# Threshold attention and Fourier mixing on one core: transposing the next pair's q and k one step earlier in the first two batches, and scaling its q at a step's end in the second

## The chip, the cores and the metric

The kernel runs on one core of a Trainium2 chip. The metric is the device time of one execution in microseconds (us). Of the kernel before there are three timed executions: 1657.55, 1662.69 and 1664.34 us, with the median 1662.69. The execution in the profile took 1657.76 us by the clock of the run and 1655.7 us from its first to its last instruction; all times "at 185.94" below are microseconds from the start of that span. A core has four engines that compute, each with its own queue: TensorE (PE, matmuls and transpositions through matmuls), VectorE (DVE), ScalarE (ACT) and GpSimd (POOL). A fifth, SyncE (SP), issues nearly all the DMAs here.

## The reference

Eight batches of eight heads, 576 tokens, 64 values a head. Scores below the row's maximum less tau are dropped before the softmax. Its output is the input of a Fourier mixing (the real part of a two-dimensional transform over tokens and over the 512 values), a normalization and two matmuls with a relu between them.

```python
scores = scale * np.matmul(q, k.transpose(0, 1, 3, 2))
thresh = np.max(scores, axis=-1, keepdims=True) - tau
scores = np.where(scores >= thresh, scores, -1000000000.0)
attn = np.exp(scores - np.max(scores, axis=-1, keepdims=True))
attn = attn / (np.sum(attn, axis=-1, keepdims=True) + 1e-09)
x = np.matmul(attn, v)                     # then (B,H,S,D) -> (B,S,H*D)
u = x + np.real(np.fft.fft(np.fft.fft(x, axis=1), axis=2))
un = (u - mean(u)) / np.sqrt(var(u) + 1e-06)
out = u + np.maximum(un @ w_ch1, 0.0) @ w_ch2
```

All arithmetic is in 32-bit floating point. The two weight matrices arrive as 64-bit values and are converted on the chip.

## The kernel before

**Pairs and steps.** Heads are worked on two at a time: 4 pairs a batch, 32 in all, numbered n. A pair has NT = 5 steps t = 0 to 4. In the first four a step takes 128 queries of both heads; the fifth (t = 4) takes the last 64 queries of both heads at once, from a small tile `q_ends`. So a batch is 20 steps (`per_batch`), and step i is step t = i mod 5 of pair n = i div 5.

**One step.** `scores` (L420) multiplies q and k into one or two PSUM tiles `sc`, of which there are two in all; L430 is the matmul of the first four steps, with the column half c in the outer loop and the head j in the inner one, L436 that of the fifth. `softmax` (L442) then takes the negated row maximum `neg` (L453, DVE), the exponential `e` (L461, ACT), the threshold `thr` (L465, ACT), the masked exponential with its row sum (L469, DVE, the last reader of the `sc` tile), and the reciprocal of the sum (L481, DVE). In the first two batches the reciprocal is spread into `rec` on GpSimd (L493). `weights_in_parts` (L504) transposes `e` on TensorE (L533, L536, L552) and ScalarE copies the result out (L540, L544, L554, L556). `weighted_values` (L561) multiplies with v, in two parts a pair (L581; L589 scales the result).

**Preparing the next pair.** `load_pair` (L124) issues eight DMAs that bring q and k of a pair, in blocks, into the tiles `q_in` and `k_in`, of which there is one each. `scale_q` (L384; L390 on GpSimd) multiplies `q_in` by 1/8. `prep_pair` (L394) makes the layout that the score matmuls want by three block transpositions on VectorE: L401 and L402 write `kT` (two buffers), L404 writes `qT` (one buffer); then it calls `load_pair` for the pair after. `prep_ends` (L409; L413 on GpSimd) copies the last 64 queries from `qT` to `q_ends`.

**Who sets the order.** In the first two batches the order of every engine is that of the program text, as the manual schedule is open from L101 to L1385. The first batch runs `step` (L1177) for i = 0 to 19. There `prep_pair(n + 1)` stands in the fifth step, after that step's `softmax`. Each step also takes one chunk of the first weight matrix through its conversion (L297 and L300 on DVE, L305, L308, L311 on ACT, L313 on DVE, L318 and L319 on GpSimd), and `busy` (L105) puts in matmuls that nobody reads. The second batch runs `second_batch` (L1313) for i = 20 to 39. It converts the second weight matrix by a list of chunks (`PLAN`), calls the Fourier mixing of the first batch (`mixing`, L653) and feeds its rows to the two matmuls of the last part (`channels`, L823, with L814 and L840) in portions: `fill` (L1161) takes as many portions as a budget allows. In its steps from the fourth on a call of `fill` stands before `transposed_weights(i - 1)`, one after the chunk stages, and one after that `prep_pair`. From the third batch on (L1388) only TensorE follows the text; a scheduler orders the other engines. There `prep_pair` stands at t = 3 already, and that loop is not touched.

In the second batch's step 22 (t = 2 of pair 4) `mix` sends GpSimd the last six additions of the Fourier mixing (L723 and L727), whose results the first matmuls of the last part (L814) need.

Of the kernel before, what the change touches and what calls it, by code (L numbers as in the profile page):

```python
# [47 lines left out]
def kernel(  # L48
# [18 lines left out]
    NT = 5  # L67
# [37 lines left out]
    def busy(n):  # L105

        for _ in range(n):
            pd = ps.tile([128, 4, 128], FP32, tag="mm", bufs=4, name="pd")
            four = bass.AP(
                tensor=ones.tensor, offset=ones.offset, ap=[list(ones.ap[0]), [0, 4], [1, 128]]  # L110
            )
            nc.tensor.matmul(pd[:, :, :], ones[:, :], four, start=True, stop=True)
# [31 lines left out]
    def load_v(n):  # L144

        b, p = n // NPAIR, PAIRS[n % NPAIR]
        vt = v_in[n % 2]
        for j in range(2):
            h = 2 * p + (j + p) % 2
            nc.sync.dma_start(  # L150
                out=vt[:, j:8:2, :], in_=v[b, h, 0:512, :].rearrange("(t p) d -> p t d", p=128)
            )
            nc.sync.dma_start(out=vt[64 * j : 64 * j + 64, 8 + j, :], in_=v[b, h, 512:576, :])
# [230 lines left out]
    def scale_q(n):  # L384

        raw = loaded[n][0]
        if n == 0:
            nc.scalar.activation(out=raw[:, :], in_=raw[:, :], func=ACT.Copy, scale=q_scale[:, :])
        else:
            nc.gpsimd.tensor_scalar(  # L390
                out=raw[:, :], in0=raw[:, :], scalar1=q_scale[:, :], scalar2=None, op0=ALU.mult
            )
# [16 lines left out]
    def prep_ends(n):  # L409

        for j in range(2):
            hp = slice(64 * j, 64 * j + 64)
            nc.gpsimd.tensor_copy(q_ends[hp, hp], heads[n][0][hp, 512:S])  # L413
# [6 lines left out]
    def scores(i):  # L420
        n, t = divmod(i, NT)
        qT, kT = heads[n][0:2]

        nh = 2 if t < 4 else 1
        sc = [ps.tile([128, 2, 512], FP32, tag="sc", name=f"sc{j}") for j in range(nh)]
        if t < 4:
            for c in range(2):
                for j in range(2):
                    hp, k0 = slice(64 * j, 64 * j + 64), D * (1 - j)
                    nc.tensor.matmul(  # L430
                        sc[j][:, c, 0:HALF], qT[hp, 128 * t : 128 * t + 128],
                        kT[hp, k0 + HALF * c : k0 + HALF * (c + 1)], start=True, stop=True,
                    )
        else:
            for c in range(2):
                nc.tensor.matmul(  # L436
                    sc[0][:, c, 0:HALF], q_ends[:, :], kT[:, D + HALF * c : D + HALF * (c + 1)],
                    start=True, stop=True,
                )
        steps[i] = (sc, nh)  # L440
# [59 lines left out]
    def transposed_weights(i):  # L500
        for _ in weights_in_parts(i):
            pass
# [58 lines left out]
    def weighted_values(n, part):  # L561

        b, p = n // NPAIR, PAIRS[n % NPAIR]
        _, _, vt, e_t, ends, recs = heads[n]
        m = (256, S - 256)[part]
        if n % NPAIR == 0 and part == 0:

            xs[b] = [None] * NPAIR
            x = xs[b][p] = sb.tile([128, m], FP32, tag="half", bufs=1, name="x_first")
        else:  # L570
            x = xs[b][p]
            if x is None or n % NPAIR == 0:
                x = sb.tile([128, S], FP32, tag=f"x{p}", bufs=1, name=f"x{p}")
            if n % NPAIR == 0:
                nc.gpsimd.tensor_copy(x[:, 0:256], xs[b][p][:, :])
            xs[b][p] = x
        cols = slice(256 * part, 256 * part + m)
        pv = ps.tile([128, 512], FP32, tag="mm", bufs=4, name="pv")
        for c in range(5):
            for j in range(2):  # L580
                nc.tensor.matmul(  # L581
                    pv[64 * j : 64 * j + 64, 0:m], vt[:, 2 * c + j, :],
                    e_t[:, 4 * j + c, 0:m] if c < 4 else ends[:, 0:m],
                    start=(c == 0), stop=(c == 4), skip_group_check=True,
                )
        if normalized(n):
            nc.scalar.copy(x[:, cols], pv[:, 0:m])  # L587
        else:
            nc.vector.tensor_tensor(  # L589
                out=x[:, cols], in0=pv[:, 0:m], in1=recs[:, 0:m], op=ALU.mult  # L590
            )
        if part == 0:
            return
        heads.pop(n)
        if p % 2:

            swap = sb.tile([2, S], FP32, tag="half", bufs=1, name="swap")
            for j in range(2):
                nc.sync.dma_start(out=swap[j : j + 1, :], in_=x[64 * j : 64 * j + 1, :])
            for j in range(2):  # L600
                nc.sync.dma_start(out=x[64 * j : 64 * j + 1, :], in_=swap[1 - j : 2 - j, :])
# [575 lines left out]
    def step(i):  # L1177

        n, t = divmod(i, NT)
        scores(i)  # L1180

        def last_stages():
            run = chunks.pop(i - 1, None)
            for _ in range(2 if run else 0):
                next(run, None)

        if t == 1 and n > 0:
            softmax(i, lambda: weighted_values(n - 1, 1), last_stages)
            load_v(n + 1)
        elif t == 3:  # L1190
            softmax(i, lambda: weighted_values(n, 0), last_stages)
        else:
            softmax(i, None, last_stages)
        if t == 1 and n > 0:
            pass
        elif later and later[0][0] <= i:
            later.pop(0)[1](i)
        else:
            busy(2 if i < NCHUNK else 1)
        if t == 2:  # L1200
            scale_q(n + 1)
        if t == NT - 1:
            prep_pair(n + 1)
        if t == 1:
            prep_ends(n)
        if i in chunks:
            next(chunks[i])
        if i > 0:
            transposed_weights(i - 1)
        if i in chunks:  # L1210
            next(chunks[i])
        while after and after[0][0] <= i:
            after.pop(0)[1]()
        if i > 0 and i + 3 < NCHUNK:
            chunks[i + 3] = w1_chunk(i + 3)
        if t == 2 and n > 0:
            folds.append(fold_rows(n - 1))
        if folds and next(folds[0], True):
            folds.pop(0)
# [93 lines left out]
    def second_batch(i):  # L1313

        nonlocal budget
        n, t = divmod(i, NT)
        first = i - per_batch
        if first != 1:
            scores(i)
        if first == 0:  # L1320

            transposed_weights(i - 1)
        softmax(i, None, lambda: (advance(first - 1), advance(first - 1)))
        chunks.pop(first - 1, None)
        transfers(first)
        fold_more()
        if t == 1:
            prep_ends(n)
        if t == 2:
            scale_q(n + 1)  # L1330
        if first == 0:
            weighted_values(n - 1, 1)
            scores(i + 1)
            column_means(LAST)
            copy_mean(LAST)
            folds.append(fold_rows(n - 1))
            while folds:
                fold_more()
            load_v(n + 1)
            start_batch(0)  # L1340
            mix(3)
            mix(3)
        elif first == 1:
            mix(3)
            transposed_weights(i - 1)
            mix(2)
            mirrored(LAST)
            for c, eng in ((1, nc.vector), (3, nc.vector), (0, nc.gpsimd), (2, nc.gpsimd)):
                less_mean(eng, LAST, c)
            advance(first)  # L1350
            advance(first)
        elif first == 2:
            mix(2)
            transposed_weights(i - 1)
            mix(2)
            weighted_values(n, 0)
            advance(first)
            advance(first)
        else:
            fill()  # L1360
            transposed_weights(i - 1)
            advance(first)
            advance(first)
            fill()
            if t == 4:
                prep_pair(n + 1)
            fill()
            if t == 2:
                weighted_values(n, 0)
            if t == 0:  # L1370
                weighted_values(n - 1, 1)
                folds.append(fold_rows(n - 1))
                load_v(n + 1)
        if first == 16:
            fold_halves(1)
        if first < 3:
            budget += 3 * per_slot
# [10 lines left out]
    for i in range(2 * per_batch, total + 1):  # L1388
# [4 lines left out]
        n, t = divmod(i, NT)  # L1393
# [79 lines left out]
```

## Time and profile before

| | us | share of the span |
|---|---|---|
| span of the profiled execution | 1655.7 | |
| TensorE busy | 1584.1 | 96% |
| VectorE busy | 1170.7 | 71% |
| ScalarE busy | 820.9 | 50% |
| GpSimd busy | 660.1 | 40% |
| one transposition L401 or L404 (128x576), median | 0.769, 0.768 | |
| one L402 (64x64), at 229.57 | 0.24 | |
| one scaling L390 in the first two batches, median | 1.73 | |

The chain of work that ended last lies on TensorE for 77% of the span, on VectorE for 14%, on ScalarE for 5% and on GpSimd for 1%. The first two batches are its mixed part: the step t = 0 of pair 8, the first of the third batch, has its scores at 305.04.

A line of a timeline gives the start, the duration, the engine, the line of the program, the operation, the tile written and the tiles read, and in brackets how long the engine had been idle before it and what ended that idle time. Adjacent matmuls of one line are merged. A line of the window table gives, for one stretch of time, how long each engine was busy.

### The profile page before, as it was taken

To read this page: it belongs to the slowest core of one execution; us is meant where nothing else is said; L and a number is where in the kernel's file an instruction comes from. 1 tells how busy PE (TensorE), PEld (TensorE's weight loads), DVE (VectorE), ACT (ScalarE), POOL (GpSimd) and SP (SyncE) were. 2 spreads that over 40 slices of the span, in tenths; PEclk is the share of its full clock that TensorE was granted. 3 is DMA by queue.
4 is the path that set the end of the run, shared out by engine and by line. 5 is a ranking of instruction groups with operands and counts; after the bars stand their busy time and mean duration, and the time that the engine had idled before them with its cause. 6 is when DMAs were issued, how large, how long until landed. Compare 5 with 4: busy or idle time off the path is not lost.

```text
span 1655.7 us, 27993 instructions
## 1 busy us (share of the span) xinstructions
PE 1584.1 (96%) x10346; PEld 1248.7 (75%) x10346; DVE 1170.7 (71%) x2518; ACT 820.9 (50%) x1786; POOL 660.1 (40%) x875
## 2 busy tenths in 40 slices
PE   8888878999999999999999999999999999999998
PEld 4545445557888787878888778887888788889998
DVE  7986776667768678776676768787786868664444
ACT  5764566444535464645353556454646455532111
POOL 6773565141431525225333253424342244215232
PEclk9999989999999999999999999999999999999999
DMA  6423221211011111100101010111101110000000
GB/s 158 122 55 111 56 83 42 43 28 29 12 35 20 25 26 29 36 16 21 28 16 35 15 35 16 42 22 22 29 15 43 22 28 1 14 4 11 13 14 14
DMA packets 203086, 57.43 MB, mean 35 GB/s; under 512 B 193827, under 2 KB 193829, under 8 KB 202950
## 3 DMA queue, kind: packets, MB, share of 16 engines
q1 hardware_dynamic: 200438, 55.34, 14.2%
q8 instruction: 82, 1.34, 0.3%
q10 hardware_dynamic: 2512, 0.30, 0.1%
q14 instruction: 54, 0.44, 0.1%
HBM read 46.02 MB, written 9.44 MB: 33 GB/s over the span
## 4 chain that ended last, share of the span: by engine, by line
PE 77%; DVE 14%; ACT 5%; issue 2%; POOL 1%; DVEq 0%; ACTq 0%; POOLq 0%
PE ph L918 23%; PE po L1082 20%; PE pv L581 9%; PE sc L430 8%; PE pw L552 5%; PE po L840 3%; DVE e L469 3%; DVE neg L453 2%; PE ph L814 2%; ACT e L461 2%; PE sc L436 1%; PE py L684 1%; PE pn L774 1%; PE pa L701 1%; DVE hs L1043 1%
## 5 line engine op out<-in xcount | busy, mean ns | idle before, releaser
L453 DVE TENSOR_REDUCE neg<-sc 128x1 f32<-128x576 f32 x288 | 207.5, 749 | 174.2 <-PE sc L430 159.9
L461 ACT ACTIVATE e<-sc,neg 128x576 f32<-128x576 f32 x288 | 212.2, 737 | 229.1 <-DVE neg L453 228.7
L469 DVE SCALAR_TENSOR_TENSOR e<-sc,thr,e 128x576 f32<-128x576 f32 x288 | 229.5, 813 | 50.5 <-ACT thr L465 49.0
L1082 PE MATMUL po<-w,hs 128*128 128x256 f32 x1024 | 246.9, 384 | 0.0
L1082 PEld LDWEIGHTS po<-w,hs 128*128 128x128 f32 x1024 | 186.7, 191 | 33.9 <-issue 12.9
L430 PE MATMUL sc<-kT,qT 64*128 64x288 f32 x1024 | 169.3, 434 | 35.0 <-DVE qT L404 27.7
L918 PE MATMUL ph<-u_t,w 128*128 128x128 f32 x1536 | 187.0, 276 | 0.0
L918 PEld LDWEIGHTS ph<-u_t,w 128*128 128x128 f32 x1536 | 179.1, 192 | 5.0 <-issue 3.7
L552 PE MATMUL pw<-ident,e 128*128 128x128 f32 x1152 | 171.2, 276 | 8.0 <-ACT y_o L689 2.3
L554 ACT COPY e_t<-pw 128x512 f32<-128x512 f32 x256 | 148.7, 594 | 49.8 <-PE pw L552 49.5
L430 PEld LDWEIGHTS sc<-kT,qT 64*128 64x128 f32 x1024 | 93.8, 188 | 98.3 <-issue 35.2
L552 PEld LDWEIGHTS pw<-ident,e 128*128 128x128 f32 x1152 | 135.7, 142 | 27.3 <-issue 4.2
L927 DVE TENSOR_TENSOR hs<-ph,hs 128x512 f32<-128x512 f32 x160 | 106.9, 685 | 69.5 <-PE ph L918 53.8
L918 PE MATMUL ph<-t_u,s_w 128*128 128x128 f32 x1024 | 126.4, 277 | 2.2 <-POOL t_u L892 1.8
L918 PEld LDWEIGHTS ph<-t_u,s_w 128*128 128x128 f32 x1024 | 119.5, 192 | 7.7 <-issue 4.9
L1082 PE MATMUL po<-hs,s_tile 128*128 128x256 f32 x512 | 121.5, 381 | 0.0
L796 DVE SCALAR_TENSOR_TENSOR u<-po,rstd,u 128x256 f32<-128x256 f32 (+1 forms) x164 | 75.3, 483 | 63.9 <-PE po L1082 62.9
L488 ACT ACTIVATE e<-e,den 128x576 f32<-128x576 f32 x96 | 74.5, 776 | 75.7 <-DVE den L481 75.3
L1082 PEld LDWEIGHTS po<-hs,s_tile 128*128 128x128 f32 x512 | 94.1, 190 | 13.7 <-issue 2.5
L935 ACT ACTIVATE hs<-hs 128x512 f32<-128x512 f32 x112 | 69.2, 630 | 62.1 <-DVE hs L927 62.1
L614 POOL TENSOR_TENSOR half<-x 128x287 f32<-128x287 f32 x48 | 40.5, 865 | 115.6 <-ACT x L587 61.0
L1078 POOL TENSOR_TENSOR hs<-hs,s_tile 128x512 f32<-128x512 f32 x32 | 42.1, 1318 | 109.4 <-PE po L1082 86.5
(196 smaller groups left out, 2911.2 us busy)
## 6 DMA issues: line engine op xcount, KB each, us to landing
hs<-in_moe_w_ch_dram SPq DMA_DIRECT2D x23, 512.0 KB, 4.5
q_in<-in_q_dram SPq DMA_DIRECT2D x128, 72.0 KB, 2.4
out_dram<-u SPq DMA_DIRECT2D x36, 256.0 KB, 2.1
k_in<-in_k_dram SPq DMA_DIRECT2D x124, 72.0 KB, 2.3
v_in<-in_v_dram SPq DMA_DIRECT2D x64, 128.0 KB, 2.3
w<-in_moe_w_ch_dram SPq DMA_DIRECT2D x6, 512.0 KB, 3.7
stage<-in_moe_w_ch_dram SPq DMA_DIRECT2D x3, 512.0 KB, 3.5
v_in<-in_v_dram SPq DMA_DIRECT2D x64, 16.0 KB, 2.1
```

The source lines that it names most:

```text
L430: nc.tensor.matmul(sc[j][:, c, 0:HALF], qT[hp, 128 * t : 128 * t + 128], kT[hp, k0 + HALF * c : k0 + HALF * (c + 1)], start=True, stop=True,)
L453: nc.vector.tensor_reduce(out=neg[:, j : j + 1], in_=sc[j][:, :, 0:HALF], axis=AXIS_XY, op=ALU.max, negate=True,)
L461: nc.scalar.activation(out=ej, in_=sc[j][:, :, 0:HALF], func=ACT.Exp, bias=neg[:, j : j + 1], scale=1.0)
L469: nc.vector.scalar_tensor_tensor(out=ej, in0=sc[j][:, :, 0:HALF], scalar=thr[:, j : j + 1], in1=ej, op0=ALU.is_ge, op1=ALU.mult, accum_out ...
L488: nc.scalar.activation(out=e[:, S : 2 * S], in_=e[:, S : 2 * S], func=ACT.Copy, scale=den[:, 1:2])
L552: nc.tensor.transpose(pw[:, c, :], e[:, c0 : c0 + 128], ident[:, :])
L554: nc.scalar.copy(e_t[:, 4 * j : 4 * j + 4, qs], pw[:, :, :])
L581: nc.tensor.matmul(pv[64 * j : 64 * j + 64, 0:m], vt[:, 2 * c + j, :], e_t[:, 4 * j + c, 0:m] if c < 4 else ends[:, 0:m], start=(c == 0), ...
L796: nc.vector.scalar_tensor_tensor(out=u, in0=product, scalar=self.rstd[:, t : t + 1], in1=u, op0=ALU.mult, op1=ALU.add,)
L918: nc.tensor.matmul(banks[name][:, 128 * q : 128 * q + 128], left[c][:, 512 * part + 128 * q : 512 * part + 128 * q + 128], right[c], start ...
L927: nc.vector.tensor_tensor(out=to, in0=bank, in1=to if other is None else other, op=ALU.add)
L1082: nc.tensor.matmul(bank[:, 0 : DM // 2], left[p], right[p], start=start and p == 0, stop=p == NK - 1, skip_group_check=True,)
```

## The change

Three edits, no operation added or taken away. In the first batch `prep_pair(n + 1)` moves from the fifth step (t = 4) to the fourth (t = 3), so that on VectorE the three transpositions stand before the fifth step's softmax instead of after it. In the second batch the same is done: the call moves from t = 4 to t = 3 at the same place inside a step, after the chunk stages and before the last `fill`. And in the second batch `prep_ends` and `scale_q` move from just after the step's softmax to the end of the step, behind whatever else that step gives to GpSimd. The purpose is to have `qT` ready before the next pair's first scores are due, and to let GpSimd do what others wait for first.

```diff
@@ step: first batch
         if t == 2:
             scale_q(n + 1)
-        if t == NT - 1:
+        if t == 3:
             prep_pair(n + 1)
@@ second_batch
         fold_more()
-        if t == 1:
-            prep_ends(n)
-        if t == 2:
-            scale_q(n + 1)
         if first == 0:
...
             fill()
-            if t == 4:
+            if t == 3:
                 prep_pair(n + 1)
             fill()
...
                 load_v(n + 1)
+        if t == 1:
+            prep_ends(n)
+        if t == 2:
+            scale_q(n + 1)
         if first == 16:
```

As `prep_pair` also loads the pair after, its eight DMAs move up in SyncE's queue with it, past one load of a weight chunk where one stands there. TensorE's order is the same in both kernels. From the third batch on a few small instructions of VectorE and ScalarE near the batch's beginning change places, because the scheduler is given another situation.

## The prediction

> **What bounds the kernel now.** I read the page first, then who waits for L404, then the windows from one pair's first scores to the next pair's, then the timelines of three engines at those boundaries. From the page, part 5:
>
> ```profile
> L430 PE MATMUL sc<-kT,qT 64*128 64x288 f32 x1024 | 169.3, 434 | 35.0 <-DVE qT L404 27.7
> ```
>
> TensorE stands idle 27.7 us in the whole run because a score matmul waits for `qT`. The line of L404, asked from 0 to 420 us alone, says where:
>
> ```profile
>   PE sc L430: 27.7, 8
> ```
>
> All 27.7 us lie in the first two batches, eight times, once for each of the pairs 1 to 8. The windows (core, engine busy times with their counts, clock granted to TensorE, DMA share) tell what those stretches are bound by:
>
> ```profile
> 39.40:70.30 30.90, 26.91 (x142) 15.52 (x142) 27.70 (x64) 23.57 (x52) 23.71 (x30) 1.00 0.43 115
> 101.30:132.20 30.90, 24.33 (x132) 14.67 (x132) 25.33 (x55) 18.61 (x43) 20.90 (x27) 0.94 0.16 30
> 185.90:230.60 44.70, 32.60 (x170) 20.12 (x170) 37.60 (x76) 29.90 (x70) 28.86 (x33) 0.91 0.30 79
> 270.60:305.00 34.40, 31.91 (x158) 18.60 (x158) 19.40 (x48) 14.68 (x37) 13.37 (x22) 0.95 0.19 35
> 305.00:340.00 35.00, 34.36 (x169) 18.43 (x170) 22.50 (x58) 18.70 (x42) 2.19 (x3) 1.00 0.23 44
> ```
>
> In the first batch VectorE (27.70 of 30.90) is fuller than TensorE; in the second they alternate; from pair 7 on TensorE leads, and after 305 it is busy 34.36 of 35.00. So time gained before 305 reaches the end undiminished, but time that TensorE alone gains in the first batch need not. The waits of the second batch in TensorE's timeline:
>
> ```profile
> 171.61 2.93 PE L814 MATMUL ph<-u_t,w 128*128 128x384 f32 x4 [3.59 <-POOL u_t L727]
> ...
> 185.94 1.24 PE L430 MATMUL sc<-kT,qT 64*128 64x288 f32 x8 [2.88 <-DVE qT L404]
> ...
> 230.66 2.29 PE L430 MATMUL sc<-kT,qT 64*128 64x288 f32 x8 [8.47 <-DVE qT L404]
> 232.88 4.51 PE L814 MATMUL ph<-u_t,w 128*128 128x384 f32 x8
> ...
> 270.60 2.29 PE L430 MATMUL sc<-kT,qT 64*128 64x288 f32 x8 [3.35 <-DVE qT L404]
> ...
> 305.04 1.24 PE L430 MATMUL sc<-kT,qT 64*128 64x288 f32 x8 [2.52 <-DVE qT L404]
> ```
>
> After the idle times of 3.35 us and more the same eight score matmuls take 2.29 us instead of 1.24, and eight of L814 4.51 instead of 2.75 (at 237.88): an idle stretch is paid twice. GpSimd's timeline ahead of 171.61:
>
> ```profile
> 164.84 1.92 POOL L390 TENSOR_SCALAR q_in<-q_in,q_scale 128x576 f32<-128x576 f32 x1
> 166.73 0.85 POOL L723 TENSOR_TENSOR u_t<-x,tmp 128x289 f32<-128x289 f32 x1
> ...
> 170.87 0.69 POOL L727 TENSOR_TENSOR u_t<-x,tmp 1x287 f32<-1x287 f32 x1
> ```
>
> The scaling of q stands without a gap before the additions that TensorE waits for. And VectorE's before 230.66:
>
> ```profile
> 225.04 0.16 DVE L481 RECIPROCAL den<-den 128x1 f32<-128x1 f32 x1
> ...
> 229.82 0.78 DVE L404 STREAM_TRANSPOSE qT<-q_in 128x576 f32<-128x576 f32 x1
> ...
> 232.98 1.42 DVE L453 TENSOR_REDUCE neg<-sc 128x1 f32<-128x576 f32 x2 [2.38 <-PE sc L430]
> ```
>
> Between softmax and transpositions stand two chunks' conversions, so the scores come 5.8 us after their tile was free (224.81), and then VectorE waits for them too.
>
> **What the Trainium skill says.** "TensorE: Matmul & The Clock Gate", Part 1, says that the clock falls to half after an idle window of about 3.4 us, that the windows run freely, and that about 3.4 us of activity bring it back; its Part 4 says that transpositions on TensorE do not count as activity in the same way. The trace agrees roughly: 3.35, 3.59 and 8.47 us of idleness were followed by halved speed, 2.52, 2.88 and 2.96 were not; and at 198.39 L814 is slow (4.45) after 3.3 us in which only transpositions ran. Its section "Architectural detail" says that VectorE and ScalarE work strictly in order and that TensorE pulls only weight loads forward. The trace agrees: at 229.82 L404 sits behind conversions, though its inputs were there. So a moved instruction delays all behind it in its queue.
>
> **The change part by part.** No operation is added. The price of the moved group is 0.77 + 0.24 + 0.78 less overlaps, 1.85 us as at 229.82 (228.79 to 230.60); L401 and L404 took 0.756 to 0.779 in all 64 cases, whatever ran beside, so it is the same in the new place.
>
> Behind the transpositions on VectorE now come the fifth step's chunk stages, its `neg`, then e on ScalarE and L469. The next pair's second score matmul (c outer, j inner) needs the `sc` tile that the fifth step's L469 frees; so the wait for `qT` becomes a wait for that L469, 2.3 us earlier in the queue than the end of L404 (129.96 against 132.2 for pair 4), later by what the transpositions push it.
>
> *Pairs 1 to 3.* VectorE is continuous through the fourth and fifth steps, so L469 is pushed by the whole 1.85 us. Pair 2: `neg` of t = 0 was at 71.59, right behind L300; it stays there. Pair 3 likewise (102.86). Pair 1 had 0.68 us of waiting for the scores at 40.68, and I get 40.2. Together 0.5 us.
>
> *Pair 4.* No chunks; VectorE is idle 1.11 us before the fifth `neg` (127.32). Transpositions from 126.2 to 128.05 push it by 0.73; L469 ends at 130.7 instead of 129.96; scores then, instead of 132.27: 1.5 gained. The PV matmuls at 135.45 took 5.5 us instead of the usual 2.9 (idle since 129); if the clock stays up, 2.6 more.
>
> *Scaling last, step 22.* L390 (1.92) leaves the place before the additions, the copies of `q_ends` (0.52, from 152.74, where they cost nothing as GpSimd idles 1.40 before 155.57) go into that gapless row: 1.4 earlier, and 1.4 more if L814 at 171.61 (2.93 instead of 1.56 at 166.46) runs at speed. L390 then ends at about 172, before the transpositions of step 23 want it at 174. The same move later in the batch hides in GpSimd's gaps (6.3 and 5.1 us at 180.93 and 189.38).
>
> *Pair 5.* The transpositions fall into VectorE's idle 5.28 us before 178.53: free. TensorE could go at 183.07 instead of 185.94 (2.9), but ScalarE is busy with conversions to 185.8, where e could have its turn, against 188.01: 2.2 gained.
>
> *Pair 6.* The transpositions push the fifth `neg` by 1.85, but ScalarE was late for it (222.97 against 221.5), so L469 moves by only 0.5, to end at 225.3. Scores at 225.4; VectorE does its two chunks to 229.25 and reads them; ScalarE is free at 231.5 instead of starting at 233.77; its copies for the PV matmuls no longer wait 2.06 us for L814 and end at 235.2. PV at 235.2 instead of 240.56: 5.3, of which about 2.8 is the slow clock.
>
> *Pair 7.* The fifth `neg` at 265.7 instead of 263.77, e pushed by 1.3 (a table load held ScalarE until 265.34), scores at 268.5 instead of 270.60: 2.1, and 1.2 from the clock: 3.3.
>
> *Pair 8.* VectorE idles 1.67 us before 299.74: pushed by 0.2. TensorE is free at 302.5, scores at 302.95 instead of 305.04: 2.1.
>
> *DMAs.* Loads of q and k are issued a step earlier, one chunk load behind them about 5 us later (SyncE issues eight in 4.3 us, at 39.38). The chunk so delayed is wanted some 6 us or more after it lands (from 2.4 to 4.5 us a load on the page). Nothing.
>
> Sum: 0.5 + 4.1 + 2.8 + 2.2 + 5.3 + 3.3 + 2.1 = 20.3 us, of which 2.6 + 1.4 + 2.8 + 1.2 = 8.0 depends on the clock. As its windows run freely, a drop may come elsewhere; I take 60% of that: 12.3 + 4.8 = 17.1.
>
> **The rivals.** *VectorE is the bound.* Then TensorE's earlier scores only wait for `neg` and e, and of the gains only those of pairs 7 and 8 remain, where VectorE has 15 us to spare: 5.4 us less, 1657. For it: 37.60 of 44.70 us for pair 5. Against it: VectorE itself waited 1.33 to 2.38 us for these scores.
>
> *The wait moves and grows (slower).* If nothing comes back because t = 0 waits for the fifth step's L469, and each of eight fifth steps is pushed by 1.85: 14.8 us, 1677; with the pushes of pairs 1 to 3 and half the others, about 1673. Against it: L469's end is before L404's in all eight.
>
> *Everything falls.* The eight waits vanish wholly, with the clock and GpSimd's part: 27.7 + 8.0 + 1.4 = 37 us, 1626. Against it: the `sc` tile is not free sooner.
>
> **How the numbers follow.** My forecast 75 in 100, VectorE as the bound 12, slower 5, everything 8. The likeliest: 1662.7 - 17.1 = 1645.6, so 1646. Low 1636: the whole sum with the clock (1642.4) and something of the third rival, less the spread of the median. High 1656: the gain without the clock (1650) and half the way to the first rival. Faster by over 0.5% (below 1654.4) is nearly all of the forecast and the third rival, 0.82; no change 0.12; slower 0.06.
>
> **What would show it.** The wait on L404 should all but vanish for pairs 1 to 8, and one on L469 of about half its size take its place; the fifth `neg` of pairs 1 to 3 should come 1.8 us later. The wait for L727 should fall from 3.59 to about 2.2, the clock's eights in the page's slices become nines, pair 8's first scores come near 288, and the time from there to the end stay at 1350.7. It is wrong if the waits reappear at `neg` and `thr` with the boundaries unmoved, or if the third batch, scheduled anew, loses what was gained.

## The result, and the profile after

| | median, us | against the kernel before on the same chip | mean clock lost a run, us |
|---|---|---|---|
| kernel before, beside the first comparison | 1662.79 (1657.55 to 1664.34) | | 22.8 |
| the change | 1635.97 (1635.02 to 1638.93) | 0.9847 [0.9822, 0.9872] | 6.5 |
| the change, once more beside later experiments | 1638.08 (1635.44 to 1638.85) | 0.9860 [0.9845, 0.9874] | 8.6 |

The last column is used below: one minus the mean granted TensorE clock, times the span. For the kernel before it is the mean of the 63 executions that stood beside the experiments.

By medians the change makes the kernel 22.5 to 26.8 us faster. The forecast was 16.7 faster, to 1646, and 1636 was the lower end of its range: the direction is right, the size too small by about a third. The profiled execution spans 1633.3 us, 22.4 less than before; the profile of the kernel before is of one of its faster executions (1657.76).

From the page of the kernel after, parts 1, 2 and 5:

```profile
PE 1580.4 (97%) x10346; PEld 1247.5 (76%) x10346; DVE 1171.1 (72%) x2518; ACT 821.4 (50%) x1786; POOL 661.8 (41%) x875
...
PEclk9999999999999999999999999999999999999999
...
L430 PE MATMUL sc<-kT,qT 64*128 64x288 f32 x1024 | 173.3, 430 | 14.5 <-DVE e L469 13.7
```

The work is the same (VectorE 1171.1 us busy, 1170.7 before). TensorE's score matmuls stood idle 14.5 us instead of 35.0, and what ends most of that is no longer `qT` but the masked exponential L469. The clock row of the page before had a single eight, which is gone:

```profile
PEclk9999989999999999999999999999999999999999
```

TensorE's idle time fell from 71.6 to 52.9 us (span less busy), its busy time by 3.7: these two make the 22.4.

Who waited for L404 after, again from 0 to 420 us:

```profile
  PE sc L430: 0.7, 1
```

Of eight waits one is left. Waits on L469 in that stretch grew from 6.6 us (12 times) to 13.2 (21 times), so 20.4 us less in all. The windows from one pair's first scores to the next pair's, the same five as before:

```profile
38.90:69.40 30.50, 27.37 (x144) 15.72 (x144) 27.41 (x64) 23.54 (x53) 22.08 (x29) 1.00 0.46 120
100.60:128.60 28.00, 24.07 (x134) 14.25 (x134) 23.79 (x55) 18.41 (x44) 21.28 (x27) 1.00 0.13 25
174.00:213.70 39.70, 33.15 (x175) 20.65 (x174) 34.88 (x73) 28.65 (x68) 26.06 (x31) 1.00 0.34 87
250.40:283.00 32.60, 31.14 (x160) 17.99 (x159) 21.25 (x54) 16.20 (x41) 13.92 (x24) 1.00 0.22 41
283.00:318.00 35.00, 34.03 (x164) 17.94 (x164) 22.07 (x58) 19.55 (x45) 2.02 (x2) 1.00 0.18 37
```

The first stretch is 0.40 us shorter than before (30.90), the one of pair 3 by 2.90, that of pair 5 by 5.00, and that of pair 7 by 1.80. The last line is the third batch's first 35 us, a length chosen for both kernels; TensorE is as full there as before (34.03 and 34.36). The clock is 1.00 in all; before it was 0.94, 0.91 and 0.95 in three of them. TensorE's timeline at the places that the prediction showed:

```profile
163.79 1.56 PE L814 MATMUL ph<-u_t,w 128*128 128x384 f32 x4 [1.75 <-POOL u_t L727]
...
173.96 1.24 PE L430 MATMUL sc<-kT,qT 64*128 64x288 f32 x8
...
211.01 0.75 PE L430 MATMUL sc<-kT,qT 64*128 64x288 f32 x2 [0.66 <-DVE qT L404]
213.68 1.21 PE L430 MATMUL sc<-kT,qT 64*128 64x288 f32 x6 [1.92 <-DVE e L469]
214.82 4.54 PE L814 MATMUL ph<-u_t,w 128*128 128x384 f32 x8
...
250.43 2.02 PE L430 MATMUL sc<-kT,qT 64*128 64x288 f32 x8
...
282.95 1.30 PE L430 MATMUL sc<-kT,qT 64*128 64x288 f32 x8
```

Pairs 5, 7 and 8 begin without a wait. Pair 6 shows what replaced the wait: the first of the step's four score matmuls (each is two in the trace) as soon as `qT` is there, then 1.92 us until L469 frees the second `sc` tile. In place of one idle stretch of 8.47 us stand two of 0.66 and 1.92, and yet L814 behind them takes 4.54: this drop of the clock stayed, as it did before at 232.88 (4.51). GpSimd's timeline ahead of 163.79, and VectorE's at the boundaries of pairs 4 and 6:

```profile
163.06 0.68 POOL L727 TENSOR_TENSOR u_t<-x,tmp 1x287 f32<-1x287 f32 x1
163.73 2.26 POOL L390 TENSOR_SCALAR q_in<-q_in,q_scale 128x576 f32<-128x576 f32 x1
```

```profile
125.19 0.78 DVE L404 STREAM_TRANSPOSE qT<-q_in 128x576 f32<-128x576 f32 x1
125.89 0.72 DVE L453 TENSOR_REDUCE neg<-sc 128x1 f32<-128x576 f32 x1
127.60 0.82 DVE L469 SCALAR_TENSOR_TENSOR e<-sc,thr,e 128x576 f32<-128x576 f32 x1 [0.99 <-ACT thr L465]
...
210.18 0.78 DVE L404 STREAM_TRANSPOSE qT<-q_in 128x576 f32<-128x576 f32 x1
210.88 0.72 DVE L453 TENSOR_REDUCE neg<-sc 128x1 f32<-128x576 f32 x1
...
212.72 0.81 DVE L469 SCALAR_TENSOR_TENSOR e<-sc,thr,e 128x576 f32<-128x576 f32 x1
```

The scaling now stands behind L727, and the transpositions ahead of the fifth `neg`. After 213.54 VectorE goes on with the next chunks and reads pair 6's first scores at 218.76 without waiting; before, it waited 2.38 us for them. The loads of q and k, which moved up too, show no part in this: up to 420 us VectorE's first transposition (L401) waited for a load once, at the start (3.4 us before, 3.3 after), and GpSimd's scaling twice (19.8 us in all before, 18.0 after).

The gain by stretches of the two profiled executions, cumulative differences taken at the end of a pair's score matmuls:

| stretch | ends at, before and after | gained | forecast with the whole clock |
|---|---|---|---|
| start to pair 3's first scores | 102.64, 101.78 | 0.9 | 0.5 |
| to pair 4's second scores | 142.11, 135.80 | 5.4 | 4.1 |
| to L814 behind L727 | 171.61, 163.79 | 1.5 | 1.4 |
| to pair 5's first scores | 187.18, 175.20 | 4.2 | 3.6 |
| to pair 6's second scores | 244.64, 227.57 | 5.1 | 5.3 |
| to pair 7's second scores | 280.81, 261.31 | 2.4 | 3.3 |
| to pair 8's first scores | 306.28, 284.25 | 2.5 | 2.1 |
| to the end | 1655.7, 1633.3 | 0.4 | 0 |
| sum | | 22.4 | 20.3 |

### The profile page after: what moved, and what is told of

Read it like the earlier page. It is cut to its first block, busy times and chain, and to the rows that moved or that the text cites. A ratio compares the mean times of both kernels' runs of the same rounds, so it can differ in the third digit from the quotient of the medians.

```text
span 1633.3 us, 27989 instructions
## 1 busy us (share of the span) xinstructions
PE 1580.4 (97%) x10346; PEld 1247.5 (76%) x10346; DVE 1171.1 (72%) x2518; ACT 821.4 (50%) x1786; POOL 661.8 (41%) x875
## 3 DMA queue, kind: packets, MB, share of 16 engines
q1 hardware_dynamic: 200438, 55.34, 14.5%
## 4 chain that ended last, share of the span: by engine, by line
PE 75%; DVE 15%; ACT 6%; issue 2%; POOL 1%; DVEq 0%; ACTq 0%; POOLq 0%
PE ph L918 24%; PE po L1082 20%; PE pv L581 9%; PE sc L430 7%; PE pw L552 5%; PE po L840 3%; DVE e L469 3%; DVE neg L453 2%; ACT e L461 2%; PE sc L436 1%; PE ph L814 1%; PE pa L701 1%; PE py L684 1%; PE pn L774 1%; DVE hs L1043 1%
## 5 line engine op out<-in xcount | busy, mean ns | idle before, releaser
L469 DVE SCALAR_TENSOR_TENSOR e<-sc,thr,e 128x576 f32<-128x576 f32 x288 | 229.4, 812 | 50.4 <-ACT thr L465 48.7
L430 PE MATMUL sc<-kT,qT 64*128 64x288 f32 x1024 | 173.3, 430 | 14.5 <-DVE e L469 13.7
L552 PEld LDWEIGHTS pw<-ident,e 128*128 128x128 f32 x1152 | 134.0, 141 | 27.7 <-ACT y_o L689 4.2
L1082 PEld LDWEIGHTS po<-hs,s_tile 128*128 128x128 f32 x512 | 94.0, 190 | 13.7 <-issue 2.5
```

The costliest lines, as they stand in the source:

```text
L430: nc.tensor.matmul(sc[j][:, c, 0:HALF], qT[hp, 128 * t : 128 * t + 128], kT[hp, k0 + HALF * c : k0 + HALF * (c + 1)], start=True, stop=True,)
L469: nc.vector.scalar_tensor_tensor(out=ej, in0=sc[j][:, :, 0:HALF], scalar=thr[:, j : j + 1], in1=ej, op0=ALU.is_ge, op1=ALU.mult, accum_out ...
L552: nc.tensor.transpose(pw[:, c, :], e[:, c0 : c0 + 128], ident[:, :])
L1082: nc.tensor.matmul(bank[:, 0 : DM // 2], left[p], right[p], start=start and p == 0, stop=p == NK - 1, skip_group_check=True,)
```

## The experiments

**Each part alone.** Four kernels, side by side: the transpositions moved in the first batch only, in the second only, the scaling (with `prep_ends`) moved only, and everything but the scaling. Their edits are pieces of the change's diff.

```diff
@@ step: first batch only (all else as before)
-        if t == NT - 1:
+        if t == 3:
             prep_pair(n + 1)
@@ second_batch only (all else as before)
-            if t == 4:
+            if t == 3:
                 prep_pair(n + 1)
@@ scaling only (all else as before); everything but the scaling is the change without this
-        if t == 1:
-            prep_ends(n)
-        if t == 2:
-            scale_q(n + 1)
         if first == 0:
...
+        if t == 1:
+            prep_ends(n)
+        if t == 2:
+            scale_q(n + 1)
         if first == 16:
```

> Only the first batch's transpositions in the fourth step, all else as before. Theory of the ledger (each boundary between pairs gives its own gain, and it reaches the end): pairs 1 to 4 give 0.5 + 4.1 by the prediction, 6.0 by the two traces, so 1657 to 1658 us. VectorE as the bound of the first batch: under 2 us, 1661 or more. The gains depend on each other through the clock's free windows: no fixed number, a sum of the parts that misses the whole by more than 5 us.

> Only the second batch's transpositions in the fourth step (pairs 5 to 8); first batch and scaling as before. Ledger: 2.2 + 5.3 + 3.3 + 2.1 = 12.9 us by the prediction, some 13 to 16 by the traces, so 1647 to 1650 us. VectorE as the bound: only pairs 7 and 8, 5.4 us, 1657. Dependence on the clock: more than 18 or under 8.

> Only the scaling of q and the copies to q_ends at the end of the second batch's steps; all transpositions as before. Ledger: 1.4 us from the shorter wait for L727 and 1.4 from the clock after it, so 1660 to 1661 us. If the boundary between pairs 4 and 5 is set by VectorE or ScalarE: nothing, 1662 to 1663.

> The change with scaling and q_ends left in their old place: both batches' transpositions in the fourth step. Ledger: the change's time and 1.4 to 2.8 us more, 1637.4 to 1639; and the gains of the two batches alone add up to this one's. But scaling now stands just ahead of the transpositions' own need of it in no case, so no new wait. If the scaling's place is worth nothing once the transpositions are early: 1636.

| moved | median, us | ratio to before | gain by medians (before: 1660.58) |
|---|---|---|---|
| first batch | 1654.92 | 0.9966 [0.9955, 0.9976] | 5.7 |
| second batch | 1645.57 | 0.9910 [0.9896, 0.9925] | 15.0 |
| scaling | 1660.29 | 0.9992 [0.9982, 1.0003] | 0.3 |
| both batches, not the scaling | 1641.19 | 0.9884 [0.9866, 0.9902] | 19.4 |

The gains of the two batches lie in the expected ranges (4.6 to 6.0 and 12.9 to 16 us; the expected times were counted from 1662.7). The two moves of transpositions add up within the intervals: 20.7 singly, 19.4 together. So the batches are nearly independent, as the forecast's sum by pairs had it. Where VectorE is the bound, only the gains of pairs 7 and 8 were to remain, and nothing of the first batch's 5.7. The scaling missed its expectation both ways: alone it is worth nothing measurable where 2.8 us were expected, and on top of the others more than 1.4 to 2.8. By medians that is 3 to 7 us (19.4 against 22.5 and 26.8), by means about 4 (20.2 against 24.2), where the change's runs stood beside other executions of the kernel before. TensorE's timeline shows a part of the reason. With the scaling alone:

```profile
170.22 2.73 PE L814 MATMUL ph<-u_t,w 128*128 128x384 f32 x4 [2.59 <-POOL u_t L727]
...
184.81 2.29 PE L430 MATMUL sc<-kT,qT 64*128 64x288 f32 x8 [3.02 <-DVE qT L404]
```

L814 comes 1.0 us sooner after its predecessors than before (2.59 against 3.59 idle), but it still runs slowly, and the scores of pair 5 then run at half speed behind the old wait for `qT`: 2.29 against 1.24 before. They come 1.1 us earlier than in the kernel before, and those of pair 6 only 0.1 (230.54 and 230.66): while the transpositions stay late, the gain is gone by then. With everything but the scaling:

```profile
168.00 1.63 PE L814 MATMUL ph<-u_t,w 128*128 128x384 f32 x4 [3.35 <-POOL u_t L727]
...
169.85 1.91 PE L552 MATMUL pw<-ident,e 128*128 128x128 f32 x8
...
171.56 3.35 PE L814 MATMUL ph<-u_t,w 128*128 128x384 f32 x8
```

the wait for L727 is nearly whole, and the slow clock comes behind it (1.91 and 3.35 instead of 1.04 and 2.75). In the first profile of the change the wait is 1.75 and what follows runs at 1.04 and 2.75. But the second profile of the same kernel has the slow clock here too:

```profile
166.02 1.70 PE L814 MATMUL ph<-u_t,w 128*128 128x384 f32 x4 [2.06 <-POOL u_t L727]
...
167.94 1.92 PE L552 MATMUL pw<-ident,e 128*128 128x128 f32 x8
...
169.65 3.28 PE L814 MATMUL ph<-u_t,w 128*128 128x384 f32 x8
```

So the scaling does not by itself keep the clock up at this place. Against this second profile the stretch from pair 4's to pair 5's first scores is 1.3 us longer without the scaling (48.4 and 47.0), as much as the wait for L727 (3.35 and 2.06). Over all executions the mean loss of clock is 11.1 us without the scaling and 7.6 with it; that the rest of the 4 us is this loss is not shown.

**The clock's part, by filling the waits.** In the kernel before, matmuls that nobody reads fill the waits for `qT` of pairs 4 to 7; the waits themselves stay. Into the kernel after, the same was put between the first and the second score matmul of pairs 5 to 8 (the second and the third of the trace's eight), where a wait for L469 can stand.

```diff
@@ scores: the kernel before, waits filled
+        for _ in range({4: 4, 5: 4, 6: 12, 7: 5}.get(n, 0) if t == 0 else 0):
+            nc.tensor.matmul(
+                sc[0][:, 0, 0:256].rearrange("p (a b) -> p a b", b=128), ones[:, :],
...
@@ scores: the kernel after, waits filled
+                    fill_in = t == 0 and c == 0 and j == 1
+                    for _ in range({5: 2, 6: 6, 7: 4, 8: 2}.get(n, 0) if fill_in else 0):
+                        nc.tensor.matmul(
...
```

> The kernel before, with matmuls that nobody reads put ahead of the first scores of pairs 4, 5, 6 and 7 (4, 4, 12 and 5 of 128x256, about 0.47 us each at full speed), so that TensorE works while it waits for qT; the transpositions stay late and the waits stay. The clock as a cost of its own: 2.6 (pair 4) + 2.8 (pair 6) + 1.2 (pair 7) = 6.6 us faster than before, about 1654, the eights of the granted clock gone after 132 us, and a smaller spread between runs. If slow matmuls after a wait are hidden by the other engines: 1660. If the clock is most of the change's gain: 1645 or less.

> The change, with such matmuls between the first and the second score matmul of t = 0 in pairs 5 to 8 (2, 6, 4 and 2), where TensorE now waits for the fifth step's masked exponential. The clock still costs 1.8 us after pair 6 and 0.8 after pair 7 in the trace of the change: up to 2.6 us faster than it, 1633.5. If the fillers push scores that the tile's release would have let go: as much slower.

The first took 1658.77 us, ratio 0.9983 [0.9973, 0.9992]: 1.8 us faster by medians and 3.0 by means, where I expected 6.6. At the four places the filling did what it should. TensorE's timeline of it (the program's lines are shifted by 6; L427 is the filling):

```profile
109.32 2.25 PE L436 MATMUL sc<-kT,qT 64*128 64x288 f32 x6 [0.20 <-DVE e L475]
...
224.59 5.35 PE L427 MATMUL sc<-ones 128*128 128x256 f32 x24
232.16 1.24 PE L436 MATMUL sc<-kT,qT 64*128 64x288 f32 x8 [2.23 <-DVE qT L404]
...
302.78 1.57 PE L436 MATMUL sc<-kT,qT 64*128 64x288 f32 x8 [2.52 <-DVE qT L404]
```

Pair 6's scores take 1.24 instead of 2.29. From a pair's first to its second scores the gain is 2.6 us for pair 4, 2.7 for pair 6 and 1.0 for pair 7, 6.3 in all, close to the 6.6 expected; nothing for pair 5, whose scores ran at full speed before too. But six scores at 109.32 now take 2.25 (1.21 before), and those at 302.78 take 1.57 (1.24). In windows of 5 us the clock is full from 130 to 145, from 225 to 240 and at 270, where it was low before, and below 0.8 at 40, 70, 110, 175 and 210, where it was full. The drops moved; the last section says what the clock's record shows of their places. Over its executions the mean loss of clock fell by 6.4 us to 16.7, the mean time by 3.0.

The second took 1638.26, ratio 0.9866 [0.9851, 0.9881], beside the change's 1638.08 on the same chip: nothing, where up to 2.6 us were expected, though its mean loss was only 5.7. The other half of the expectation came true: the filling also pushed scores that had not waited. At pair 7 (lines shifted by 8; L432 is the filling):

```profile
252.51 0.75 PE L438 MATMUL sc<-kT,qT 64*128 64x288 f32 x2
253.19 1.99 PE L432 MATMUL sc<-ones 128*128 128x256 f32 x8
255.11 1.23 PE L438 MATMUL sc<-kT,qT 64*128 64x288 f32 x6
```

The first scores of pairs 5 to 8 take 3.0, 4.7, 3.8 and 3.0 us in its profile and 1.2, 3.9, 2.0 and 1.3 in the change's. L814 behind pair 6 is quick again (2.85 instead of 4.54). From pair 8's first scores to the end its profile takes 1353.6 us against 1350.4; why is open. So this filling gains nothing, and it does not tell what the clock alone still costs the change.

**What a loss of clock costs.** The 63 executions of the kernel before beside these experiments run from 1657.2 to 1665.6 us. Time and lost clock go together: correlation 0.95, slope 0.61 us of time for one us lost, and 1647.3 us at no loss. A correlation does not say which causes which, as a longer wait can also bring the clock down. The filling, which changed the clock at chosen places, gives 3.0 us for 6.4, or 0.47. Much of the slow work lies where TensorE would have waited anyway: the second profile of the change has 8.5 us more lost by windows of 5 us up to 350 us (10.2 against 1.7), TensorE 6.6 us longer busy (1587.0), its waits on L469 3.5 us shorter (10.2 against 13.7 on the page), and a span 3.3 us longer: 0.39 for one us lost.

**More transpositions, late and early.** The three transpositions of pairs 1 to 8 are made twice, once in the kernel before and once in the kernel after, so that the group costs 1.85 us more in its old and in its new place.

```diff
@@ prep_pair, behind the three transpositions
+        if 1 <= n <= 8:
+            nc.vector.transpose(kT[:, D : D + S], k_raw[:, :])
+            nc.vector.transpose(kT[64:128, 0:D], k_raw[64:128, 512:S])
+            nc.vector.transpose(qT[:, :], q_raw[:, :])
```

> The kernel before, with the three block transpositions of pairs 1 to 8 made twice, one after the other, still behind the fifth step's softmax: one more group of 1.85 us of VectorE in front of every one of the eight waits for qT. My theory (these transpositions set the moment of the next pair's first scores, as long as they stand behind the softmax): all eight are paid in full, 14.8 us, and a few us more because longer waits bring the clock down more often: 1676 to 1680 us beside 1660.6. The rival that VectorE's whole work bounds the first two batches expects the same 14.8 here, and the same in the early place too. A rival that the transpositions hide beside other work expects under 5.

> The kernel after the change, with the three transpositions of pairs 1 to 8 made twice, in the new place ahead of the fifth step's softmax. My theory: the added 1.85 us are paid in full only where VectorE is continuous through the fourth and fifth steps (pairs 1 to 3), and for the most part in pairs 4, 6, 7 and 8, whose slack the first group has used up; in pair 5, where VectorE idled over 5 us, nothing. So 7 x 1.85 = 13 at most, less what ScalarE hides in pair 6: 8 to 13 us above the change, 1646 to 1651 us. The rival that VectorE's whole work bounds expects 14.8, as in the late place; the rival that the early place is free expects 0 to 3.

Late: 1676.06 us beside 1661.08, ratio 1.0093 [1.0077, 1.0109]: 15.0 more, at the lower end of what was expected. Early: 1654.96, ratio 0.9962 [0.9950, 0.9975]: 17 to 19 us more than the change, well over the 8 to 13 expected. From the two pages, late and then early (the program's lines are shifted by 4):

```profile
L434 PE MATMUL sc<-kT,qT 64*128 64x288 f32 x1024 | 176.8, 448 | 46.1 <-DVE qT L408 40.4
```

```profile
L434 PE MATMUL sc<-kT,qT 64*128 64x288 f32 x1024 | 175.5, 435 | 23.5 <-DVE e L473 20.3
```

The scores' idle time grew by 11.1 us late (46.1 against 35.0) and by 9.0 early (23.5 against 14.5): in waits, the early place did cost what I expected, while late not all eight were paid in full (the waits for `qT` grew by 12.7, not 14.8). Most of the rest goes with the clock, which my expectation for the early place had left out: the mean loss rose by 6.2 us to 29.3 late, and by some 11 us to 18.8 early, worth 3.8 and 6.9 us at the slope above. TensorE's timeline of the early one:

```profile
72.29 2.29 PE L434 MATMUL sc<-kT,qT 64*128 64x288 f32 x6 [1.75 <-DVE e L473]
...
107.64 1.21 PE L434 MATMUL sc<-kT,qT 64*128 64x288 f32 x6 [2.16 <-DVE e L473]
...
185.55 1.24 PE L434 MATMUL sc<-kT,qT 64*128 64x288 f32 x8
```

Pair 2's six scores run at half speed. Pair 5 begins without a wait even with two groups ahead of it; its stretch is 1.6 us longer than in the change, but that is L814 and the transpositions on TensorE from 174.06 to 178 (2.43 and 1.68 instead of 1.56 and 1.04). So pair 5's slack of over 5 us was real. At each of the other seven boundaries the scores waited longer than in the change, by 0.4 to 2.1 us. By the totals alone the rival that VectorE's whole work bounds (14.8 in both places) does better here than my range. It falls by the change itself, which moved that work and gained over 22, and by pair 5's missing wait; for added work in the first batch it says the same as my reading.

**A better place for four of the eight.** In the first batch VectorE is continuous up to the fifth `neg`, but then waits for ScalarE's `thr` (1.09, 0.39 and 0.86 us in the change's profile, ahead of pairs 1, 2 and 3). This kernel puts the transpositions for pairs 1 to 3, and for pair 7, into that gap, between `neg` and L469; the other four stay as in the change.

```diff
@@ step: first batch, between neg and the masked exponential of the fifth step
             for _ in range(2 if run else 0):
                 next(run, None)
+            if t == 4 and n + 1 < 4:
+                prep_pair(n + 1)
...
-        if t == 3:
+        if t == 3 and n + 1 == 4:
             prep_pair(n + 1)
@@ second_batch: the same for n + 1 == 7
```

> The change, but for pairs 1, 2, 3 and 7 the three transpositions stand in the fifth step between its maximum and its masked exponential, where VectorE waits for ScalarE anyway. If the fifth step's masked exponential sets the boundary, it is pushed by 1.85 us less that wait, in place of 1.85: 1.0 + 0.5 + 0.6 + 1.3 = 3.4 us faster than the change, about 1632.6. If VectorE's whole work bounds the first batch, the order inside it does nothing: 1635 to 1636.

It took 1633.43 us (1633.31 to 1633.55), ratio 0.9834 [0.9822, 0.9847], beside 1635.44 to 1638.85 for the change on the same chip: 4.7 us faster by medians (3.4 expected), and the fastest kernel of this study. VectorE's timeline at pair 1:

```profile
33.89 0.76 DVE L453 TENSOR_REDUCE neg<-sc 128x1 f32<-128x576 f32 x1
...
36.22 0.78 DVE L404 STREAM_TRANSPOSE qT<-q_in 128x576 f32<-128x576 f32 x1
36.92 0.78 DVE L469 SCALAR_TENSOR_TENSOR e<-sc,thr,e 128x576 f32<-128x576 f32 x1
```

L469 comes at 36.92 without a gap; in the change it comes at 37.93 after 1.09 us of waiting. By pair 3's first scores the profile is 2.8 us ahead of the change's (98.97 against 101.78), at pair 8's 2.3: in between it fell back to 1.3 at pair 6 (1.27 at its second scores), with the clock at 0.79 and 0.87 in the windows from 160 to 170, where the change's profile had the full clock, and from pair 6 to pair 7 it gained 1.0 again.

## Why the forecast was right in direction and short in size

**The waits.** That the wait on `qT` gives way to a shorter one on L469 holds at pairs 1 to 4 and 6 (1.44, 1.30, 0.55, 0.33 and 1.92 us, at pair 6 behind 0.66 on `qT`); pairs 5, 7 and 8 have no wait of either kind before their first scores. Pair 4: L404 was to be done before the fifth `neg`, which it was to push by 0.73; in the traces the fourth step's `neg` comes 2.12 us earlier (121.89 and 119.77) and the fifth's 1.43 (127.32 and 125.89), so the push is 0.7. The scores of pair 4 come 3.70 earlier (132.27 and 128.57), 1.6 more than the 2.12 that the fourth step handed on (forecast 1.5). Pair 6: L469 was to end at 225.3 by the old count; it ends at 213.54, and with the 11.98 gained by then that is 225.5. Scaling: 1.4 forecast, 1.5 gained, and L390's end, 165.99, is 172.3 to 173.8 by the old count (forecast 172).

The signs came in part with other sizes. The wait on L469 was to take half the old wait's place, about 14 us; it grew by 6.6. And L727's wait fell to 1.75, or 2.06 in the second profile (forecast about 2.2). The fifth `neg` of the first three pairs was to come 1.8 us later and comes 1.4 to 1.5 later from the start of the span, which is 1.6 to 1.8 later behind the fourth step's softmax. The clock's eights were one eight, and it became a nine. Pair 8's scores were to be near 288 and are at 282.95. From there to the end it takes 1350.35 us against 1350.7: the third batch lost nothing.

**The step that fell short is the clock's term**, "I take 60% of that": 4.8 of 8.0 us. The mean loss of clock was 22.8 us before and 7.6 after (6.5 and 8.6), 15.2 less. At the slope of 0.61 that is worth 9.3 us, and the waits are the rest of the mean gain of 24.2: 14.9 instead of 12.3. The clock's 4.5 us are then nearly two thirds of the 7.1 that were missing. The slope is a regression over executions of the kernel before, carried over to the change; it isn't a separate measurement. With the filling's 0.47 the clock is worth 7.1 and the waits 17.1, with the 0.39 of the two profiles 5.9 and 18.3. So the waits' term, 12.3, was too small as well; how the missing part divides between the two stays open.

Of that step the traces show this. The 8.0 us counted only slow matmuls behind the waits that the change removes. Two more are slow in the first profile before and not in the first after: matmuls of L112 at 116.80, at the end of pair 3, took 2.07 us before and 1.13 after, and L814 at 198.39 took 4.45. The first can explain 0.9 of the 1.3 us by which pair 4's stretch beat its forecast. But such a drop is not tied to the change: the profile of the change with its waits filled, the same program up to pair 5's first scores, has the low clock again from 116.1. So this part of the two profiles' difference is chance. A discount for drops that come elsewhere was right for filling four waits (6.3 us gained at the places, 1.8 to 3.0 in the end). For the change fewer came back: its mean loss is 7.6 us against 16.7 with the waits filled. The last section gives a likely reason, as the change leaves fewer stretches in which TensorE is nearly idle; no experiment tested that by itself.

**The rivals.** VectorE as the bound (1657) falls: the first batch alone gains 5.7. The wait that grows (1673 to 1677) falls: 20.4 us of waits on `qT` and L469 are gone. Everything falls (1626) is too much: waits of 13.2 us on L469 and 1.8 on L727 are left. The range's lower end was set by hand from part of that last rival, and the first median, 1635.97, lies on it.

**Pairs 1 to 3** gained 0.9 where 0.5 was forecast, though the waits on L404 there were 7.5 us (27.7 less the five of pairs 4 to 8): the push of L469 takes nearly all back. Of the 0.9, 0.3 stood already at the very first scores (9.89 and 9.61). The experiment with the transpositions inside the softmax shows what that push cost: 2.8 us between two single profiles.

## What to carry to other kernels

When a preparation stands between two users on an in-order engine, ask of each place what it pushes there: the same 1.85 us cost nothing where the engine had slack (pair 5), nearly its whole gain where the engine was continuous (pairs 1 to 3), and less again inside the gap in which the engine waits for its partner. Take the clock as part of a wait's price, but count it over the whole stage and over many executions, not at the place of one wait in one trace. And where several waits lie close together, a part that measures nothing alone can be worth about 4 us with the others.

## What the runs showed of the hardware

- The spread of one kernel's time, 1657 to 1666 us, goes with the clock: correlation 0.95 over 63 executions, 0.61 us of time for one us of lost clock. Filling waits gave 0.47, two profiles of the change 0.39.
- Drops of the clock have no fixed places, but they lie on a grid. In the clock records of the twelve profiles (before, after and ten experiments, each without its last 20 us) all 79 drops last 3.41, 6.83 or 10.24 us, and in each profile they begin on one grid of 3.41 us. In the kernel before they begin at 116.80, 133.87, 171.41, 198.72, 226.02 and 270.40: 5, 11, 8, 8 and 13 such windows apart. The grid lies differently in each execution. Up to 350 us the kernel after the change lost clock only at 215 in one profile, and at 21, 41, 72, 109, 167 and 219 in another.
- How busy TensorE is in one window goes with the clock in the next. In the twelve profiles a drop followed each of the 37 full-speed windows in which TensorE was busy for less than 40% of the time, and none of the 5402 with 70% or more; of the 149 between, 42 were followed by one, and what decides there is open. Up to 330 us there were three windows of under 40% before, none and one in the two profiles after, and four with the waits filled. Where a wait falls on the grid matters beside its length: in the kernel before the 3.35 us ahead of pair 7 fell into one window (8% busy), and a drop followed; the 2.96 us ahead of pair 2 fell across two (51% and 62%), and none did.
- One long idle stretch isn't needed. In the profile after, the window from 211.80 was 45% busy, its longest idle time was 1.92, and the drop at 215.22 followed. "TensorE: Matmul & The Clock Gate", Part 1, of the Trainium skill speaks of an idle window of about 3.4 us; here such a window was partly busy.
- Transpositions on TensorE counted as work. The prediction took the slow L814 at 198.39, and the page that it names, to mean that they count less. In 26 full-speed windows the other matmuls filled at most 40%, and only with the transpositions was TensorE busy for 60% or more: no drop followed. The window ahead of 198.72 was 48% busy in all.
- VectorE's conversions of 128x512 vary severalfold at one shape: L297 took 0.41 us at 173.92 and 1.51 at 216.91, L300 0.41 at 208.80 and 2.01 at 160.55, all in one execution of the kernel after. What made the difference is open. The block transpositions hardly varied (0.76 to 0.78).
